# Convolution taps summed by accumulating DMAs, with matmul operands at round SBUF addresses

## The chip, the cores and the metric

The kernel runs on one core of a Trainium2 chip. Five engines work side by side: TensorE (PE, matmuls; PEld is its weight load), VectorE (DVE), ScalarE (ACT), GpSimd (POOL) and SyncE (SP, which here issues DMAs). The metric is the device time of one execution in microseconds, lower is better; the time before is the median of 3 runs.

## What is computed

A short causal convolution over the sequence (7 taps, one softmaxed set of taps for each of 8 groups of 24 channels), then a two-layer feed-forward with a clipped quadratic between its layers:

```python
x: (8, 4096, 192)   weight: (8, 7)   w_in: (192, 2048)   w_out: (2048, 192)
w = softmax(weight)                                     # over the 7 taps
conv[b, s, h, :] = sum_k w[h, k] * x_pad[b, s + k, h, :]  # 6 zeros in front
h = conv.reshape(32768, 192) @ w_in
g = where(h >= 1, h, where(h <= -1, 0, (h + 1)**2 / 4))
out = g @ w_out
```

## The kernel before

**Tiles and steps.** The 32,768 tokens form 64 blocks of 512 (`TB`), and `s` counts them. Each block has 8 steps (`NPAIR`), one for each 256 columns of the hidden layer, so the main loop runs over `q` = 0 to 511, and two more turns. In a step PE does the first layer for `q` (`mm1`, line 390) and the second layer for `q - 2` (`mm2`, line 430). The 192 channels are cut as 128 + 64, and every matmul is cut into two of 64 rows that run on the two halves of the array at once. Here such two are called a pair. From block 1 in the first layer, and from step 16 in the second, each operand is split into a high and a low part of type fp32r (`hi`/`lo`, `gh`/`gl`, `w`), and three products of parts are summed. A full step is 9 pairs in `mm1` and 10 in `mm2`, all with 512 columns. The moving operand of a pair is one row of 512 floats (2,048 bytes) in each partition: the convolved tokens in `mm1` (pool `xo`), `gh` and `gl` in `mm2` (pool `act`). The stationary operand is 128 floats (512 bytes) in each partition of `w0` to `w9` and `wr2` to `wr9` (pool `const`). In the first steps the operands are plain fp32, and lines 408 and 426 run on whole values.

**Between the layers.** For each `q`: DVE clips `h` from PSUM (line 463), ACT squares (469), DVE takes the maximum with `h` (474), and one step later ACT rounds to `gh` (481) and DVE subtracts to `gl` (487). After each block ACT copies four accumulators out, POOL adds them (501, 512), DVE transposes and SP stores.

**The convolution.** It is made for two blocks at a time, a unit `c` of 16 steps (`i` = 0 to 15), and ahead of its use. A unit has three parts, called B (the first 128 channels of the odd block), A (those of the even block) and R (the last 64 channels of both). Each part goes through: DVE transposes the loaded tokens to `xT` (147, "T" in the tables); ACT multiplies tap 0 into `y` (226); for each of taps 1 to 6 ACT makes a product `p` (219) and POOL adds it to `y` (230); "split" then makes the parts that matmuls read: ACT casts `y` to `hi` (248; for R `rh`, 262), POOL (for R DVE) subtracts to `lo`, and SP's DMAs copy both with the halves swapped. A and R made in unit `c` serve unit `c + 1`; B serves its own unit from `i` = 8 on. Three tables, `PLAN_B`, `PLAN_A` and `PLAN_R`, say at which `i` which taps are done; they are read in the order B, A, R, at the end of each step's work on ACT, POOL and DVE. All engines work their queues in order. Tiles `xT` and `y` have two buffers, `p` three. The first unit has tables of its own (`FIRST_...`) and another path (line 129), which the change leaves alone.

**Where tiles lie.** Pools are laid out in SBUF in the order in which they are opened, and tiles within a pool in the order in which they are first asked for. `w0` starts at byte 16,512 of each partition, which is 128 above a multiple of 512, and so do all parts of `w` and `wr`. All tiles of `xo`, `act` and `ob` start 448 bytes above a multiple of 1,024.

Of the kernel before, what the change touches and what calls it, by code (L numbers as in the profile page):

```python
# [8 lines left out]
F32 = mybir.dt.float32  # L9
# [5 lines left out]
ALU = mybir.AluOpType  # L15
# [3 lines left out]
P = 128  # L19
# [11 lines left out]
def lightconv_then_ffn(ctx: ExitStack, tc: tile.TileContext, x, weight, w_in, w_out, out):  # L31
# [24 lines left out]
    nc = tc.nc  # L56
    B, S, D = x.shape
    H, K = weight.shape
# [12 lines left out]

    const = ctx.enter_context(tc.tile_pool(name="const", bufs=1))
    stage = ctx.enter_context(tc.tile_pool(name="stage", bufs=2))
    xin = ctx.enter_context(tc.tile_pool(name="xin", bufs=3))
    xw = ctx.enter_context(tc.tile_pool(name="xw", bufs=2))
    xo = ctx.enter_context(tc.tile_pool(name="xo", bufs=3))
    act = ctx.enter_context(tc.tile_pool(name="act", bufs=2))
    ob = ctx.enter_context(tc.tile_pool(name="ob", bufs=2))
    ps_h = ctx.enter_context(tc.tile_pool(name="ps_h", bufs=2, space=PSUM))
    ps_o = ctx.enter_context(tc.tile_pool(name="ps_o", bufs=1, space=PSUM))  # L80
    ctx.enter_context(tc.manual_schedule())
# [53 lines left out]
    class Conv:  # L135
# [86 lines left out]
        def taps(self, *ks):  # L222
            y = self.y
            for k in ks:
                if k == 0:
                    nc.scalar.mul(y, self.xT[:, SH:SH + TB], wk[:, self.wsel, 0:1])
                elif self.c == 1 and self.u != "b":
                    pending.append((y, y, self.product(k)))
                else:
                    nc.gpsimd.tensor_add(y, y, self.product(k))  # L230

        def swapped(self, t, name, bufs):

# [35 lines left out]
        def split_halves(self):  # L269
# [26 lines left out]
    wo_w = w_out.bitcast(U32).rearrange("(f p) (d two) -> p f d two", p=P, two=2)  # L296
    n_in = [CI if j < NPAIR else 0 for j in range(NCH)]
    n_all = [n_in[j] + (CO if j >= LAG else 0) for j in range(NCH)]
    W = [const.tile([P, 2, n_in[j] + (CW if j >= LAG else 0)], F32R, name=f"w{j}")
         for j in range(NCH)]  # L300
    CC = max(n_all)
# [12 lines left out]
    class Chunk:  # L314
# [51 lines left out]
        def parts(self, rest):  # L366
            j, k = self.j, n_in[self.j]
            if rest:
                yield (WF[j][:, :, 0:P],
                       *(W[j][:, i, k:].rearrange("p (f d) -> p f d", f=2) for i in range(2)))  # L370
                yield WF[j][:, :, P:], WR[j][:, :, 0], WR[j][:, :, 1]
            else:
                yield WI[j], W[j][:, 0, 0:k], W[j][:, 1, 0:k]

# [15 lines left out]
    def mm1(q):  # L390
# [11 lines left out]
        else:  # L402
            mms = [(W[j][:, part], u + u, [xop[s][u, x]] * 2) for u in "nsr"
                   for part, x in ((0, "hi"), (1, "hi"), (0, "lo"))]
# [25 lines left out]
    def mm2(q):  # L430

        s, j = divmod(q, NPAIR)
        gh, gl = ghs.pop(q), gls.pop(q)
        w, wr, k = W[j + LAG], WR[j + LAG], n_in[j + LAG]
        if j == 0:
# [131 lines left out]
                    in_=y[i][:, 0:2 * D].rearrange("p (b d) -> p b d", b=2))  # L567


    wk = const.tile([P, 2, K], F32, name="wk")  # L570
    warm = const.tile([P, 1], F32, name="warm")
    whose = const.tile([P, 2 * P + 3 * K + 3], F32, name="whose")[:, 0:2 * P]
    one = ob.tile([P, TB], F32, name="sum")[:, 0:P]
    small, busy = (ob.tile([P, TB // SQ, SQ], F32, name="osb").rearrange("p j b -> p (j b)")
                    for _ in range(2))
# [118 lines left out]

    PLAN_B = {0: (0, 1), 2: (2, 3), 3: (4, 5), 4: (6,), 5: "split"}
    PLAN_A = {4: ("T", 0), 5: (1, 2), 6: (3, 4), 7: (5, 6), 8: "split"}
    PLAN_R = {7: ("T",), 8: (0, 1, 2), 10: (3, 4), 11: (5, 6), 13: "split"}


    FIRST_B = {2: 2, 3: 3, 4: 4, 5: 5}
# [4 lines left out]
    def conv_slot(i, b, a, r):  # L707
        early = b.c == 0
        plans = ((None if early else b, PLAN_B), (a, FIRST_A if early else PLAN_A),
                 (r, FIRST_R if early else PLAN_R))  # L710
        for u, plan in plans:
# [201 lines left out]
```

## Time and profile before

| | us |
|---|---|
| median of 3 runs | 2256.68 |
| lowest, highest | 2256.22, 2258.37 |
| span of the profiled execution, first to last instruction | 2255.6 |
| PE busy | 2249.6 |
| DVE busy | 2103.2 |
| ACT busy | 1697.6 |
| POOL busy | 1168.4 |

An engine's busy time is the time in which at least one of its instructions runs. The records of matmuls include the time in which a result drains out of the array, so successive ones overlap and a busy PE says nothing of the rate: that is read from how many matmuls end up in a stretch of time. A group's row gives the count, the busy time, the mean of one in ns, and the idle time of the engine just before them with what ended it. In a row of stretches each engine's busy time stands with the number of its instructions that touch the stretch.

### The profile page before, as it was taken

The numbers are of one execution on the slowest core, as the hardware profiler recorded it, in microseconds if no ns is written. First come the engines' busy times: TensorE is split into PE (matmuls) and PEld (weight loads), VectorE is DVE, ScalarE is ACT, GpSimd is POOL, SyncE is SP. The second block draws the span as 40 slices with busy tenths as digits, with TensorE's granted clock in tenths as the row PEclk, the third lists the DMA queues.
The fourth block names the chain that finished last, engine by engine and source line by source line (L and its number), as shares of the span: only waits on it lengthen the run. The fifth ranks groups of instructions, "written<-read, shape, count | busy, mean of one in ns | idle before, by whom it ended". The sixth has DMA issues, their size and how long they took to land.

```text
span 2255.6 us, 48202 instructions
## 1 busy us (share of the span) xinstructions
PE 2249.6 (100%) x19645; PEld 1842.2 (82%) x19645; DVE 2103.2 (93%) x1883; ACT 1697.6 (75%) x2153; POOL 1168.4 (52%) x868
## 2 busy tenths in 40 slices
PE   9999999999999999999999999999999999999999
PEld 6988888888888888888888888888888888888887
DVE  8899999999999999999999999999999999999997
ACT  7677877778777787777877777877778777787775
POOL 1446644556445565454654455644556545565441
PEclk9999999999999999999999999999999999999999
DMA  7222222222222212222222222222222222212211
GB/s 158 49 51 48 42 46 47 51 53 39 51 49 46 53 34 51 49 49 51 41 46 47 49 51 51 39 49 46 49 53 39 51 49 46 54 35 50 49 34 24
DMA packets 442125, 110.84 MB, mean 49 GB/s; under 512 B 410288, under 2 KB 417840, under 8 KB 441904
## 3 DMA queue, kind: packets, MB, share of 16 engines
q1 hardware_dynamic: 441744, 107.66, 25.8%
q8 instruction: 155, 2.54, 0.5%
q14 instruction: 66, 0.54, 0.1%
q10 hardware_dynamic: 160, 0.10, 0.0%
HBM read 32.84 MB, written 25.17 MB: 26 GB/s over the span
## 4 chain that ended last, share of the span: by engine, by line
PE 100%; ACT 0%; DVE 0%; issue 0%; DVEq 0%; POOL 0%; POOLq 0%; ACTq 0%
PE h L408 47%; PE accm L452 30%; PE accr L452 20%; PE accr L426 1%; PE accm L426 1%; PE accr L190 0%; PE accm L602 0%; PE accr L408 0%; PE accm L181 0%; PE h L155 0%; PE h L553 0%; PE accr L646 0%; ACT xT L168 0%; ACT xT L165 0%; ACT xT L167 0%
## 5 line engine op out<-in xcount | busy, mean ns | idle before, releaser
L230 POOL TENSOR_TENSOR y<-y,p 128x512 f32<-128x512 f32 x546 | 765.5, 1402 | 730.8 <-DVE g L474 559.5
L487 DVE TENSOR_TENSOR gl<-g,gh 128x1024 fp32r<-128x1024 f32 (+1 forms) x497 | 732.1, 1473 | 27.6 <-ACT gh L481 23.6
L469 ACT ACTIVATE g<-g 128x1024 f32<-128x1024 f32 (+1 forms) x505 | 535.3, 1060 | 242.4 <-DVE g L463 232.9
L463 DVE TENSOR_SCALAR g<-h 128x1024 f32<-128x1024 f32 (+1 forms) x505 | 609.8, 1208 | 97.1 <-PE h L408 88.1
L481 ACT CAST gh<-g 128x1024 fp32r<-128x1024 f32 (+1 forms) x497 | 521.7, 1050 | 237.1 <-DVE g L474 225.6
L408 PE MATMUL h<-hi,w 64*128 64x512 f32 x4032 | 629.8, 389 | 0.0
L474 DVE TENSOR_TENSOR g<-h,g 128x1024 f32<-128x1024 f32 (+1 forms) x505 | 613.4, 1215 | 12.1 <-ACT g L469 4.5
L452 PE MATMUL accm<-gh,w 64*128 64x512 f32 x3966 | 535.0, 388 | 0.0
L408 PEld LDWEIGHTS h<-hi,w 64*128 64x128 f32 x4032 | 382.6, 184 | 81.9
L452 PEld LDWEIGHTS accm<-gh,w 64*128 64x128 f32 x3966 | 372.3, 184 | 81.8 <-issue 0.2
L408 PE MATMUL h<-lo,w 64*128 64x512 f32 x2016 | 399.6, 388 | 0.0
L219 ACT ACTIVATE p<-xT,wk 128x512 f32<-128x512 f32 x562 | 375.1, 710 | 0.0
L452 PE MATMUL accm<-gl,w 64*128 64x512 f32 x1984 | 308.1, 388 | 0.0
L452 PE MATMUL accr<-gl,wr 64*128 64x512 f32 x1984 | 308.0, 388 | 0.0
L452 PE MATMUL accr<-gh,wr 64*128 64x512 f32 x1984 | 308.0, 388 | 0.0
L408 PE MATMUL h<-rh,w 64*128 64x512 f32 x992 | 306.0, 388 | 0.0
L408 PE MATMUL h<-rhi,w 64*128 64x512 f32 x992 | 306.0, 388 | 0.0
L408 PEld LDWEIGHTS h<-lo,w 64*128 64x128 f32 x2016 | 193.3, 184 | 41.5 <-DMA lo<-lo 0.3
L501 POOL TENSOR_TENSOR sum<-t 128x512 f32<-128x512 f32 (+1 forms) x124 | 160.7, 1316 | 126.3 <-ACT t L499 126.3
L452 PEld LDWEIGHTS accm<-gl,w 64*128 64x128 f32 x1984 | 186.4, 184 | 40.9
L452 PEld LDWEIGHTS accr<-gh,wr 64*128 64x128 f32 x1984 | 186.4, 184 | 40.9
L452 PEld LDWEIGHTS accr<-gl,wr 64*128 64x128 f32 x1984 | 186.4, 184 | 40.9
(145 smaller groups left out, 1976.8 us busy)
## 6 DMA issues: line engine op xcount, KB each, us to landing
out_dram<-osb SPq DMA_DIRECT2D x366, 64.0 KB, 2.0
raw<-in_x_dram SPq DMA_DIRECT2D x334, 68.0 KB, 2.4
hi<-hi SPq DMA_DIRECT2D x126, 128.0 KB, 2.3
lo<-lo SPq DMA_DIRECT2D x126, 128.0 KB, 2.3
rhi<-rh SPq DMA_DIRECT2D x62, 128.0 KB, 2.2
rlo<-rl SPq DMA_DIRECT2D x62, 128.0 KB, 2.3
words<-in_moe_w_in_dram SPq DMA_DIRECT2D x16, 192.0 KB, 4.0
words<-in_moe_w_out_dram SPq DMA_DIRECT2D x8, 384.0 KB, 5.0
```

The costliest lines, as they stand in the source:

```text
L219: nc.scalar.mul(p, self.xT[:, SH + k:SH + k + TB], wk[:, self.wsel, k:k + 1])
L230: nc.gpsimd.tensor_add(y, y, self.product(k))
L408: nc.tensor.matmul(h[e], w[HALVES[e], c0:c0 + P], x[e][e], start=(n == 0), stop=(n == len(mms) - 1))
L426: nc.tensor.matmul(accs[s][a, i][:, c0:c0 + D], g[half, e, b * P:(b + 1) * P], w[half, e, :], start=(j == 0 and e == 0 and b % 2 == 0), st ...
L452: nc.tensor.matmul(accs[s][a, i], st, g[HALVES[i], e, :], start=(j == 0 and n == first[a]), stop=(j == NPAIR - 1 and n == last[a]))
L463: nc.vector.tensor_scalar(out=g[:, e, :], in0=hs[q][:, e, :], scalar1=-1.0, scalar2=1.0, op0=ALU.max, op1=ALU.min)
L469: nc.scalar.activation(g[:, e, :], g[:, e, :], AF.Square, bias=0.5, scale=0.5)
L474: nc.vector.tensor_tensor(out=g[:, e, :], in0=h[:, e, :], in1=g[:, e, :], op=ALU.max)
L481: nc.scalar.copy(gh[:, e, :], gs[q][:, e, :])
L487: eng.tensor_sub(gl[:, e, :], g[:, e, :], gh[:, e, :])
L501: nc.gpsimd.tensor_add(y[:, n], t[0][:, n], t[1][:, n])
```

## The change

Two things are changed.

**The adds.** Line 230's add on POOL becomes a DMA issued from POOL's queue that reads `p` and adds it onto `y` in SBUF (`accum_op`). The three tables are spread: mostly one tap a step for each part instead of two, B's split moves from `i` = 5 to 6, A's from 8 to 10, R's from 13 to 14; A's transpose comes at 2 instead of 4.

**The addresses.** Pools `xw` and `xin`, whose tiles have odd sizes (`xT` and `raw` are 2,176 bytes), are opened after `ob`; `warm` and `wk` are asked for before the weights, with `warm` at 320 bytes; `whose` loses 96 bytes. With that `w0` starts at 16,896, a multiple of 512, as do all parts of `w` and `wr`, and all tiles of `xo`, `act` and `ob` start at multiples of 1,024. No matmul is added, removed or moved.

```diff
-    xin = ctx.enter_context(tc.tile_pool(name="xin", bufs=3))
-    xw = ctx.enter_context(tc.tile_pool(name="xw", bufs=2))
     xo = ctx.enter_context(tc.tile_pool(name="xo", bufs=3))
     act = ctx.enter_context(tc.tile_pool(name="act", bufs=2))
     ob = ctx.enter_context(tc.tile_pool(name="ob", bufs=2))
+    xw = ctx.enter_context(tc.tile_pool(name="xw", bufs=2))
+    xin = ctx.enter_context(tc.tile_pool(name="xin", bufs=3))
...
                 else:
-                    nc.gpsimd.tensor_add(y, y, self.product(k))
+                    nc.gpsimd.dma_start(out=y, in_=self.product(k), accum_op=ALU.add)
...
+    warm = const.tile([P, 80], F32, name="warm")[:, 0:1]
+    wk = const.tile([P, 2, K], F32, name="wk")
     W = [const.tile([P, 2, n_in[j] + (CW if j >= LAG else 0)], F32R, name=f"w{j}")
...
-    wk = const.tile([P, 2, K], F32, name="wk")
-    warm = const.tile([P, 1], F32, name="warm")
-    whose = const.tile([P, 2 * P + 3 * K + 3], F32, name="whose")[:, 0:2 * P]
+    whose = const.tile([P, 2 * P], F32, name="whose")
...
-    PLAN_B = {0: (0, 1), 2: (2, 3), 3: (4, 5), 4: (6,), 5: "split"}
-    PLAN_A = {4: ("T", 0), 5: (1, 2), 6: (3, 4), 7: (5, 6), 8: "split"}
-    PLAN_R = {7: ("T",), 8: (0, 1, 2), 10: (3, 4), 11: (5, 6), 13: "split"}
+    PLAN_B = {0: (0, 1), 1: (2,), 2: (3,), 3: (4,), 4: (5, 6), 6: "split"}
+    PLAN_A = {2: ("T", 0), 3: (1,), 4: (2,), 5: (3,), 6: (4,), 7: (5,), 8: (6,), 10: "split"}
+    PLAN_R = {7: ("T", 0), 8: (1,), 9: (2,), 10: (3,), 11: (4,), 12: (5, 6), 14: "split"}
```

How the queues change is shown at two places of a unit in the middle of the program. The first is POOL's queue from B's tap 1 (`i` = 0) to B's split. A row is a line of the program, an operation, what it writes and reads, and the semaphores that it waits for (DMASW are those of POOL's own DMAs, DMAHW those of SP's, the others name engines). Before:

```order
L230 TENSOR_TENSOR y<-y,p 128x512 [waits Activation_49]
L501 TENSOR_TENSOR sum<-t 128x512 [waits DVE_49,Activation_49] x2
L230 TENSOR_TENSOR y<-y,p 128x512 [waits Activation_49,Pool_49] x2
L512 TENSOR_TENSOR sum<-sum,t 64x512 [waits Activation_49]
L230 TENSOR_TENSOR y<-y,p 128x512 [waits Activation_49,Pool_49] x3
L252 TENSOR_TENSOR lo_8797<-y,hi_8796 128x512 [waits DMAHW4_49,DMAHW5_49,PE_49,Activation_49]
```

And after:

```order
L230 DMA y<-p 128x512 [waits Activation_49,Pool_49]
L503 TENSOR_TENSOR sum<-t 128x512 [waits DVE_49,Activation_49] x2
L230 DMA y<-p 128x512 [waits DMASW0_49,Activation_49]
L230 DMA y<-p 128x512 [waits DMASW1_49,Activation_49]
L514 TENSOR_TENSOR sum<-sum,t 64x512 [waits Activation_49]
L230 DMA y<-p 128x512 [waits DMASW2_49,Activation_49]
L230 DMA y<-p 128x512 [waits DMASW7_49,DVE_49,Activation_49]
L230 DMA y<-p 128x512 [waits DMASW3_49,Activation_49]
L230 DMA y<-p 128x512 [waits DMASW5_49,Activation_49]
L230 DMA y<-p 128x512 [waits DMASW4_49,Activation_49]
L230 DMA y<-p 128x512 [waits DMASW7_49,Activation_49]
L252 TENSOR_TENSOR lo_8853<-y,hi_8852 128x512 [waits DMAHW4_49,DMASW6_49,DMAHW5_49,PE_49,Activation_49]
```

The six adds of B are now six DMAs, each of which waits for the landing of the one before it on the same `y`; between them stand A's taps 1, 2 and 3. In the third and fourth row from below, B's tap 6 waits for tap 5, which was issued just before it, and A's tap 2 stands behind that wait.

The second place is ACT's queue from B's taps 5 and 6 to its split. Before:

```order
L219 ACTIVATE p<-xT,wk 128x512
L219 ACTIVATE p<-xT,wk 128x512 [waits Pool_49]
L481 CAST gh<-g 128x1024 [waits DVE_49,PE_49]
L469 ACTIVATE g<-g 128x1024 [waits DVE_49]
L219 ACTIVATE p<-xT,wk 128x512 [waits Pool_49]
L226 ACTIVATE y<-xT,wk 128x512 [waits DVE_49]
L481 CAST gh<-g 128x1024 [waits PE_49]
L469 ACTIVATE g<-g 128x1024 [waits DVE_49,Activation_49]
L248 CAST hi_8796<-y 128x512 [waits DMAHW3_49,DMAHW2_49,Pool_49]
```

And after:

```order
L219 ACTIVATE p<-xT,wk 128x512 [waits DMASW2_49,Activation_49]
L219 ACTIVATE p<-xT,wk 128x512 [waits DMASW3_49,Activation_49]
L219 ACTIVATE p<-xT,wk 128x512 [waits DMASW4_49,Activation_49]
L483 CAST gh<-g 128x1024 [waits DVE_49,PE_49]
L471 ACTIVATE g<-g 128x1024 [waits DVE_49]
L219 ACTIVATE p<-xT,wk 128x512 [waits DMASW5_49,Activation_49]
L483 CAST gh<-g 128x1024 [waits DVE_49,PE_49]
L471 ACTIVATE g<-g 128x1024 [waits DVE_49]
L248 CAST hi_8852<-y 128x512 [waits DMAHW3_49,DMAHW2_49,DMASW6_49]
```

B's cast to `hi` now waits for the landing of a DMA (tap 6) instead of for POOL's add, and stands two steps behind the products of taps 5 and 6. Each product also waits for the landing of a DMA: the one that last read its `p` buffer.

## The prediction

> **What bounds the kernel now.** I read the page's head and its chain of work first, then the granted clock.
>
> ```profile
> span 2255.6 us, 48202 instructions
> PE 2249.6 (100%) x19645; PEld 1842.2 (82%) x19645; DVE 2103.2 (93%) x1883; ACT 1697.6 (75%) x2153; POOL 1168.4 (52%) x868
> PE 100%; ACT 0%; DVE 0%; issue 0%; DVEq 0%; POOL 0%; POOLq 0%; ACTq 0%
> core 0: 2255.6 us, clock 1.000
> ```
>
> The chain that ended last lies on PE alone, at the full clock. So nothing that DVE, ACT, POOL or a DMA does is on the path now; only the pace of PE's matmuls is. That pace is not to be had from busy times. I take it from counts in long stretches (the columns: stretch, length, then each engine's busy time with its instructions; last the clock, the DMA share and GB/s).
>
> ```profile
> 200.00:1200.00 1000.00, 1000.00 (x8742) 819.97 (x8740) 942.39 (x806) 759.03 (x947) 536.08 (x385) 1.00 0.26 47
> 1200.00:2200.00 1000.00, 1000.00 (x8742) 819.98 (x8740) 941.77 (x806) 759.25 (x948) 537.02 (x382) 1.00 0.25 46
> 200.00:2200.00 2000.00, 2000.00 (x17480) 1639.95 (x17478) 1884.15 (x1611) 1518.28 (x1895) 1073.10 (x767) 1.00 0.26 47
> 104.00:2248.00 2144.00, 2144.00 (x18738) 1758.02 (x18736) 2013.71 (x1725) 1619.03 (x2017) 1134.23 (x811) 1.00 0.25 46
> ```
>
> The two halves together count 4 matmuls more than the whole, so each stretch counts 4 that only reach into it. 2000 us hold 17,476 half matmuls, 8,738 pairs: **228.9 ns a pair**, alike in both halves. 19 pairs make a step of 4.349 us. From 104 us to the end it is 18,734 / 2 = 9,367 pairs.
>
> Is 228.9 ns what 512 columns must take? The first steps run on plain fp32, with other column counts (columns of the timeline: start, length, engine, line, what, count):
>
> ```profile
> 15.27 1.88 PE L408 MATMUL h<-hi,gh 64*128 64x512 f32 x8
> 16.98 1.02 PE L408 MATMUL h<-rh,gh 64*128 64x512 f32 x4
> 17.84 1.88 PE L408 MATMUL h<-hi,gh 64*128 64x512 f32 x8
> 19.56 1.02 PE L408 MATMUL h<-rh,gh 64*128 64x512 f32 x4
> 20.41 0.82 PE L426 MATMUL accm<-wf,g 64*128 64x192 f32 x8
> 21.07 0.82 PE L426 MATMUL accr<-wf,g 64*128 64x192 f32 x8
> 21.71 0.82 PE L426 MATMUL accm<-wf,g 64*128 64x192 f32 x8
> 22.36 0.82 PE L426 MATMUL accr<-wf,g 64*128 64x192 f32 x8
> ```
>
> 12 pairs of 512 columns go from 15.27 to 20.41 us, 428.3 ns each; 12 pairs of 192 columns from 20.41 to 22.36 us, 162.5 ns each. The 320 columns between them cost 265.8 ns, 0.831 ns a column, and 162.5 - 192 x 0.831 leaves 3.0 ns fixed for a matmul. An fp32r pair needs 228.9 ns for the same 512 columns, about half, so I take it to stream at twice that rate: 512 x 0.4153 + 3.0 = **215.7 ns** (an estimate from these rows). Measured is 13.2 ns more, and it is there in every stretch. A gain must come out of these 13.2 ns, or there is none.
>
> The Trainium skill, "TensorE: Matmul & The Clock Gate", section "Back-to-back issue gap", gives N / 2.4 + 2.5 ns for successive matmuls, 215.8 ns at 512. The first steps' 3.0 ns agree with its fixed part, the 228.9 ns do not; by that page's gap the sum below would be 122 us instead of 124.
>
> **The change part by part.**
>
> *Addresses.* What could 13.2 ns be? A row of 512 floats is 2,048 bytes, read at 4 bytes per 0.4153 ns; 13.2 ns are then 127 bytes. The rows begin at 448 bytes above a multiple of 1,024, which is 3.5 x 128: if the array's reads go by blocks of 128 bytes, a row touches 17 of them where 16 would do, and one block more costs 13.3 ns. In the first steps a block lasts twice as long in the array as it takes to read, which would hide it there. At multiples of 1,024 the row has 16 blocks. The weights start at 128 above a multiple of 512, already whole blocks of 128, and load beside the matmuls (PEld 82%), so I expect nothing from their move. The cost of a matmul by address is nowhere in the trace of before, since every fp32r row lies at the same offset. The bounds are 13.2 ns less a pair and, if the new offsets were the worse ones, as much more: 9,367 x 13.2 ns = 124 us either way. I take the whole gain, because bytes and time agree within 1%: **-124 us**.
>
> *DVE, once PE is faster.* A step of 19 x 215.7 ns is 4.098 us. DVE is busy 1884.15 of 2000 us, 4.097 us a step: it would have nothing left. Here the adds matter.
>
> ```profile
> L487 DVE TENSOR_TENSOR gl<-g,gh 128x1024 fp32r<-128x1024 f32 x495 | 730.8, 1476 | 27.1 <-ACT gh L481 23.2
> L474 DVE TENSOR_TENSOR g<-h,g 128x1024 f32<-128x1024 f32 x503 | 612.2, 1217 | 12.1 <-ACT g L469 4.5
> L230 POOL TENSOR_TENSOR y<-y,p 128x512 f32<-128x512 f32 x546 | 765.5, 1402 | 730.8 <-DVE g L474 559.5 <-ACT p L219 147.7
> L501 POOL TENSOR_TENSOR sum<-t 128x512 f32<-128x512 f32 x122 | 158.7, 1321 | 123.3 <-ACT t L499 123.3
> L512 POOL TENSOR_TENSOR sum<-sum,t 64x512 f32<-64x512 f32 x61 | 138.3, 2268 | 1.5 <-ACT t L511 1.5
> L252 POOL TENSOR_TENSOR lo<-y,hi 128x512 fp32r<-128x512 f32 x62 | 81.1, 1308 | 144.4 <-ACT hi L248 144.4
> ```
>
> The subtraction to `gl` takes 1,476 ns, the maximum over as many elements 1,217. The timeline shows why: the subtraction that meets an add of POOL is slower.
>
> ```profile
> 998.73 1.30 POOL L230 TENSOR_TENSOR y<-y,p 128x512 f32<-128x512 f32 x1 [19.04 <-DVE g L474]
> 1000.51 1.22 DVE L487 TENSOR_TENSOR gl<-g,gh 128x1024 fp32r<-128x1024 f32 x1
> 1002.78 2.56 POOL L501 TENSOR_TENSOR sum<-t 128x512 f32<-128x512 f32 x2 [2.75 <-ACT t L499]
> 1004.86 1.56 DVE L487 TENSOR_TENSOR gl<-g,gh 128x1024 fp32r<-128x1024 f32 x1
> ```
>
> Without line 230, 158.7 + 138.3 + 81.1 = 378 of POOL's 1,144 us are left, a third, so of the 259 ns of excess I keep 86: DVE 0.173 us less a step, 3.92 of 4.098 us or 96%, where it has 94% now and holds up nothing. For the odd step with two transposes I add **+2 us**. The adds' own 765.5 us of POOL are off the path: nothing.
>
> *The DMAs.* 546 of them, 256 KB each.
>
> ```profile
> hi<-hi SPq DMA_DIRECT2D x126, 128.0 KB, 2.3
> words<-in_moe_w_out_dram SPq DMA_DIRECT2D x8, 384.0 KB, 5.0
> q1 hardware_dynamic: 441744, 107.66, 25.8%
> 1008.20 0.86 SPq L528 DMA_DIRECT2D out_dram<-osb  x2
> L219 ACT ACTIVATE p<-xT,wk 128x512 f32<-128x512 f32 x562 | 375.1, 710 | 0.0
> ```
>
> An accumulating one isn't in the trace. From issue to landing I bound it by 2.3 us (half the bytes, within SBUF) and 5.0 us (1.5 times the bytes, from DRAM, while the start loads everything), and take 3.0, near the first, which is the same kind of copy. The Trainium skill, "DMA: Bandwidth & Descriptors", section "Anatomy of one DMA", has about 2 us plus bytes / 436e3 for POOL's path, 2.6 us here; with it too the chains below fit. Issuing one costs POOL between the 0.43 us of SP's and the 1.30 us of an add, so POOL gets no busier. The load: 143 MB more beside 107.66 MB at 25.8% is 60% at most at the same cost per byte.
>
> What waits? POOL's queue stands behind tap 6's wait for tap 5 (A's tap 2 is behind it), and ACT's cast to `hi` in `i` = 6 waits for tap 6. From the start of tap 5's product in `i` = 4 to that cast are two steps, 8.20 us at the faster pace; less the product's 0.71 us, 7.5 us for two landings, 3.75 each. At 3.0 us there are 1.5 us to spare: nothing. R's taps 5 and 6 in `i` = 12 and its cast in 14 have the same distance. Single taps have a whole step, 4.1 us, each.
>
> **The sum.** 2255.6 - 124 + 2 = 2133.6 us of span; the median lies 1.1 us above this execution's span: **2135 us**.
>
> **The rivals.**
>
> *No effect of addresses.* The 13.2 ns belong to an fp32r matmul as such. For it: they are the same for all pairs in every stretch; against it: nothing but their size. Then PE stays the bound, the relief of DVE and POOL is off the path, and the time is 2256 us. The Trainium skill, "SBUF — State Buffer", section "Specifications (TRN2)", knows lines of 16 bytes; 448 is a multiple of 16, so by that page the move gives nothing. No row of before can decide it.
>
> *Half an effect*, the weights' reads or another block size holding the rest: about 2197 us.
>
> *Late chains: slower.* Where an accumulation takes longer than 3.75 us, ACT's in-order queue stands at the two casts, and behind it the square and `gh` that the next `mm2` needs. With L us to land, each of 31 units loses up to 2 x (2L - 7.5) us, less what ACT's idle quarter takes back. At L = 5.0, the upper bound, that is 155 us: 2290 us even with the full gain. Slower begins at L = 4.7. For it: 256 KB are read twice and written. Against it: the 2.3 us of the nearest copy.
>
> *Worse offsets: slower.* Weights and rows now begin at the same 512-byte phase; if that made them collide, up to +124 us, 2380 us.
>
> **How the numbers follow.** Forecast 0.45, half an effect 0.08, no effect 0.27, late chains 0.14, worse offsets 0.06. Faster by over 0.2% (what a measurement here can tell from no change) is 0.53; within it 0.26, a little of "no effect" falling outside; slower 0.21. The range takes in the forecast, with up to 15 us below for a smaller fixed part, the half effect and no effect, 0.80 together: 2120 to 2262 us. The forecast's own range is 2125 to 2160, the upper end for DVE as the bound.
>
> **What would show it.** Right: some 18,730 matmuls in 2,022 us, a pair at 215.7 ns, the first steps unchanged; the subtraction near 1.3 us; no idle time of ACT's casts on a DMA. Wrong: a pair still at 228.9 ns (no effect); PE with idle time behind `gh` or `hi` (late chains); PE idle behind DVE (the relief was too small).

## The result, and the profile after

The changed kernel takes **2479.08 us** (median of 4 runs, 2467.35 to 2487.02) against 2256.55 of before: 1.098 times the time, 95% interval 1.095 to 1.101. It is slower by a tenth, where I had forecast 2135 us.

The head of the page of after, its chain of work and its clock, in the order in which I read them before:

```profile
span 2485.2 us, 48615 instructions
PE 2%; issue 0%; DMA 0%; SPq 0%; POOL 0%; DVE 0%; ACT 0%; DVEq 0%; POOLq 0%
core 0: 2485.2 us, clock 0.972
```

The chain can be followed back through 2% of the span only, and DMAs and POOL stand in it: PE is no longer the one engine behind the end. The granted clock is down to 0.972. If PE had work all the time, the full clock would make the 2485.2 us about 70 us shorter (2485.2 x 0.028, an estimate). Who waits for what stands in the view of waits (engine, tile and line, the releaser, us in total, times, longest):

```profile
POOL y L230 <- DMA y<-p: 622.7, 232, 5.4
...
ACT rh L262 <- DMA y<-p: 75.3, 30, 5.2
...
ACT p L219 <- DMA y<-p: 53.8, 60, 1.8
...
PE h L410 <- DMA lo<-lo: 36.9, 29, 3.2
PE h L410 <- POOL lo L252: 35.4, 28, 2.8
...
PE h L410 <- DMA rhi<-rh: 20.4, 22, 2.4
PE h L410 <- DMA rlo<-rl: 16.5, 30, 0.7
...
PE accm L454 <- ACT gh L483: 9.2, 12, 1.3
```

Once a unit (there are 31) the first layer waits for the low part of B, and once a unit for R's two parts. Behind both stand the landings of the new DMAs: the cast to `rh` waits for one directly, and POOL's queue waits for one 232 times. The page's row on them, with KB each and the median time from issue to landing, and the queue's row (packets, MB, share):

```profile
y<-p POOLq DMA_DIRECT2D x546, 256.0 KB, 3.4
q0 software_dynamic: 78624, 143.17, 32.3%
```

3.4 us, not 3.0; one in twenty takes over 4.8 us. One unit shows how that becomes idle time of PE. POOL's timeline, then a piece of the timeline with PE, ACT and SP beside it (start, length, engine, line, what, count, and in brackets the idle time before it):

```profile
1113.27 0.86 POOL L230 DMA_DIRECT2D y<-p  x1 [2.35 <-DMA y<-p]
1117.00 1.76 POOL L230 DMA_DIRECT2D y<-p  x2 [2.87 <-ACT g L471]
1123.26 0.86 POOL L230 DMA_DIRECT2D y<-p  x1 [4.51 <-ACT gh L483]
1123.82 1.64 POOL L252 TENSOR_TENSOR lo<-y,hi 128x512 fp32r<-128x512 f32 x1
```

```profile
1120.53 0.60 ACT L248 CAST hi<-y 128x512 fp32r<-128x512 f32 x1
...
1123.13 0.61 PE L410 MATMUL h<-hi,w 64*128 64x512 f32 x4
...
1125.49 0.46 SPq L235 DMA_DIRECT2D lo<-lo  x1
...
1125.52 0.50 PE L410 MATMUL h<-lo,w 64*128 64x512 f32 x2 [1.77 <-POOL lo L252]
1125.85 0.63 PE L410 MATMUL h<-hi,w 64*128 64x512 f32 x4
...
1127.72 1.60 PE L410 MATMUL h<-lo,w 64*128 64x512 f32 x2 [1.24 <-DMA lo<-lo]
```

B's cast to `hi` ends at 1121.13. POOL could subtract `lo` then, but A's tap 3 stands ahead in its queue and waits for A's tap 2, the second issue in the 1.76 us row at 1117.00. The bracket at 1123.26 names ACT's cast, which is one of several things that this instruction waits for; in the trace tap 2 is issued at 1117.53 and lands 5.2 us later, at 1122.73, and tap 3 follows it by 0.53 us. So `lo` starts at 1123.82, 2.7 us late, and PE, which has reached the step that reads it, stands twice: first for `lo` itself, then for its copies. The windows view of the same place (stretch, length, five engines' busy time with counts, clock, DMA share, GB/s) shows the second half of the price:

```profile
1127.20:1128.50 1.30, 0.78 (x1) 0.28 (x1) 0.00 (x0) 0.68 (x1) 0.67 (x1) 0.50 0.53 123
1128.50:1131.50 3.00, 2.99 (x15) 2.41 (x16) 0.86 (x1) 0.00 (x0) 0.75 (x1) 0.50 0.46 83
...
1136.00:1141.00 5.00, 5.00 (x47) 5.00 (x46) 3.99 (x4) 3.40 (x6) 1.47 (x3) 1.00 0.55 99
```

The granted clock is 0.50 in the second gap and for some microseconds behind it, and the matmuls that do run take about twice as long. The trace of before has no such stretch.

For everything below I use one ledger. The trace gives the time from the first matmul of `mm1` in a step to that of the next step. Less 19 pairs at the kernel's own undisturbed spacing, that is what the step lost, the cost of the half clock included. The mean over units 1 to 30 of the profiled execution, by `i`:

| kernel | median us | lost, us a unit | at `i`=0 (R) | at `i`=6 | at `i`=8 (B) |
|---|---|---|---|---|---|
| before | 2256.6 | 0.05 | 0.01 | 0.00 | 0.00 |
| after | 2479.1 | 8.20 | 1.88 | 1.10 | 5.08 |
| addresses alone | 2235.7 | 0.05 | 0.01 | 0.00 | 0.00 |
| tables, adds on POOL | 2260.6 | 0.86 | 0.10 | 0.00 | 0.70 |
| DMAs and tables, old addresses | 2525.5 | 8.83 | 2.30 | 1.43 | 4.83 |
| only B by DMA | 2336.4 | 3.32 | 0.12 | 0.04 | 2.78 |
| only A by DMA | 2251.1 | 0.65 | 0.01 | 0.00 | 0.00 |
| only R by DMA | 2280.2 | 1.44 | 1.38 | 0.00 | 0.00 |
| `lo` on DVE | 2472.5 | 7.54 | 2.44 | 1.19 | 3.15 |
| half of each tap by DMA | 2418.3 | 5.76 | 0.31 | 0.07 | 5.21 |
| half, and `lo` on DVE | 2346.5 | 3.82 | 0.39 | 0.10 | 2.17 |

The steps between lose next to nothing in the changed kernel: three places hold 8.06 of its 8.20 us.

### The profile page after: what moved, and what is told of

Read it like the earlier page. It is cut to its first block, busy times and chain, and to the rows that moved or that the text cites. A ratio compares the mean times of both kernels' runs of the same rounds, so it can differ in the third digit from the quotient of the medians.

```text
span 2485.2 us, 48615 instructions
## 1 busy us (share of the span) xinstructions
PE 2352.8 (95%) x19645; PEld 1935.0 (78%) x19645; DVE 2047.4 (82%) x1883; ACT 1698.8 (68%) x2153; POOL 821.7 (33%) x868
## 5 line engine op out<-in xcount | busy, mean ns | idle before, releaser
L230 POOL DMA_DIRECT2D y<-p x546 | 474.1, 919 | 1385.7 <-DMA y<-p 622.7
L489 DVE TENSOR_TENSOR gl<-g,gh 128x1024 fp32r<-128x1024 f32 (+1 forms) x497 | 674.4, 1357 | 121.8 <-ACT gh L483 117.6
L410 PE MATMUL h<-hi,w 64*128 64x512 f32 x4032 | 747.4, 388 | 4.2 <-DMA hi<-hi 4.2
L410 PE MATMUL h<-lo,w 64*128 64x512 f32 x2016 | 606.4, 398 | 73.6 <-DMA lo<-lo 36.9
L454 PE MATMUL accm<-gh,w 64*128 64x512 f32 x3966 | 658.3, 401 | 9.8 <-ACT gh L483 9.2
L410 PEld LDWEIGHTS h<-hi,w 64*128 64x128 f32 x4032 | 538.7, 185 | 70.8 <-DMA hi<-hi 6.3
L454 PEld LDWEIGHTS accm<-gh,w 64*128 64x128 f32 x3966 | 471.9, 191 | 89.8 <-ACT gh L483 21.2
L410 PEld LDWEIGHTS h<-lo,w 64*128 64x128 f32 x2016 | 349.5, 186 | 140.0 <-DMA lo<-lo 61.5
L454 PE MATMUL accm<-gl,w 64*128 64x512 f32 x1984 | 416.1, 400 | 2.0 <-DVE gl L489 0.3
L454 PE MATMUL accr<-gh,wr 64*128 64x512 f32 x1984 | 407.7, 393 | 0.0
L410 PEld LDWEIGHTS h<-rhi,w 64*128 64x128 f32 x992 | 182.0, 188 | 49.2 <-DMA rhi<-rh 31.4
```

Source lines behind the costliest of these rows:

```text
L230: nc.gpsimd.dma_start(out=y, in_=self.product(k), accum_op=ALU.add)
L410: nc.tensor.matmul(h[e], w[HALVES[e], c0:c0 + P], x[e][e], start=(n == 0), stop=(n == len(mms) - 1))
L454: nc.tensor.matmul(accs[s][a, i], st, g[HALVES[i], e, :], start=(j == 0 and n == first[a]), stop=(j == NPAIR - 1 and n == last[a]))
L489: eng.tensor_sub(gl[:, e, :], g[:, e, :], gh[:, e, :])
```

## The experiments

### Addresses, DMAs and tables apart

The new addresses, with line 230's add and the three tables of before:

```diff
-                    nc.gpsimd.dma_start(out=y, in_=self.product(k), accum_op=ALU.add)
+                    nc.gpsimd.tensor_add(y, y, self.product(k))
```

> The new addresses with the adds on POOL and the old tables, so no accumulating DMA. Theory S (the addresses are worth 2.2 ns a pair, as the changed kernel's 226.67 ns in its undisturbed stretches say): 9,367 pairs x 2.2 ns = 21 us off 2256.6, about 2236 us, ratio 0.991, PE in the chain throughout, clock 1.00. Rival T (the addresses are worth the forecast 13.2 ns, and 143 MB of DMA traffic beside the matmuls hides most of it in the changed kernel): pairs at 215.7 ns, about 2135 us. Rival D (the pairs are faster but DVE, at 942 of 1000 us, can't follow): above 2240 us with PE waiting for DVE.

2235.73 us, ratio 0.991 (0.989 to 0.992): theory S to the microsecond, and **faster than both kernels**, 0.9% below before. Its windows and the clock:

```profile
200.00:1200.00 1000.00, 1000.00 (x8828) 826.47 (x8826) 946.29 (x814) 763.01 (x955) 538.82 (x385) 1.00 0.25 48
1200.00:2200.00 1000.00, 1000.00 (x8828) 826.46 (x8826) 944.11 (x811) 762.41 (x954) 540.45 (x383) 1.00 0.24 46
```

8,824 half matmuls in 1000 us are 4,412 pairs, 226.65 ns each (the records, in whole ns, give 226.67). The gain is 2.2 ns a pair, not 13.2, and no DMA traffic hid the rest.

The DMAs and the spread tables in the kernel of before:

```diff
-                    nc.gpsimd.tensor_add(y, y, self.product(k))
+                    nc.gpsimd.dma_start(out=y, in_=self.product(k), accum_op=ALU.add)
```

> The accumulating DMAs and the spread tables at the old addresses. Theory C (the loss is the late chains: a landing of 3.4 us and 0.5 us to the next issue leave single taps no slack): pairs at 228.9 ns where nothing disturbs, PE waiting for the lo and rh parts as in the changed kernel, about 2256.6 + 240 = 2490 to 2500 us, some 20 us more than the changed kernel's. Rival (the loss comes from the new addresses, or from both together): near 2257 us.

2525.52 us, ratio 1.119 (1.117 to 1.120). The loss is the DMAs' and tables'; it comes out 25 us above the top of what I expected, with the same three places in the ledger.

The changed kernel with line 230's add alone put back, so that only tables and addresses differ from before:

> The new addresses and the spread tables, but each tap added by POOL. Theory C: the spread tables do no harm by themselves, so the time is that of the addresses alone, 2236 us within 5 us, and no part is late. Rival (the tables put the parts too late whoever adds): more than 2300 us, PE waiting for the lo parts and for rh.

2260.60 us, ratio 1.002 (1.001 to 1.003). A miss for both theories: the tables do cost, 24.9 us over the addresses alone, most of it ahead of B's low part. PEld's wait in this run:

```profile
PEld h L410 <- DMA lo<-lo: 19.6, 33, 1.7
```

Here no accumulating DMA exists. B is late because its split stands in `i` = 6 instead of 5. Counted from the start of `mm1` in `i` = 6, the mean times in B's path (units 1 to 29) are:

| kernel | `hi` ends | `lo` starts | `lo` ends | `mm1` of `i`=8 starts |
|---|---|---|---|---|
| addresses alone | 1.71 | 1.79 | 3.09 | 8.61 |
| tables, adds on POOL | 6.08 | 6.16 | 7.46 | 8.61 |
| only B by DMA | 7.74 | 8.18 | 9.47 | 8.85 |
| `lo` on DVE | 7.96 | 8.49 | 9.17 | 9.83 |
| half of each tap by DMA | 6.49 | 8.84 | 10.38 | 8.68 |
| half, and `lo` on DVE | 6.49 | 7.40 | 8.44 | 8.74 |
| after | 7.85 | 9.80 | 11.44 | 9.72 |

After `lo` come two copies on SP, the second issued 0.5 us behind the first; with the tables alone it lands 3.0 us after the end of `lo` in the mean. The third pair of `mm1` reads `lo` itself, but the copies are read first by the sixth pair, at 8.61 + 5 x 0.227 = 9.74 us. So `lo` must end by about 6.7 us. The old table leaves 3.6 us to spare; the new one is 0.76 us late before a DMA has taken any time, which is close to the 0.70 us of the ledger.

### One part at a time by DMA

In each of these kernels one part keeps its DMAs and its new table; the others are added by POOL. With A or R alone, the other two also have their old tables back; with B alone, they keep the new ones. The edit for B:

```diff
-                    nc.gpsimd.dma_start(out=y, in_=self.product(k), accum_op=ALU.add)
+                    if self.u == "b":
+                        nc.gpsimd.dma_start(out=y, in_=self.product(k), accum_op=ALU.add)
+                    else:
+                        nc.gpsimd.tensor_add(y, y, self.product(k))
```

> The changed kernel with A's and R's taps added by POOL again; only B's six taps are DMAs. In the changed kernel PE loses 5.1 us a unit ahead of the low part of B, 1.1 us two steps before, and 2.0 us ahead of R's. Theory C1 (B's own chain of six landings is too long): the 5.1 us stay, about 2235 + 31 x 5.1 = 2390 us. Rival C2 (it is the other parts' taps in POOL's queue, and their waits, that hold B up): the gap ahead of B's low part is down to the 0.7 us of the tables alone, about 2260 us. R's loss goes in both.

2336.37 us, ratio 1.034 (1.033 to 1.036), between the two. Ahead of B's low part PE loses 2.78 us a unit: 0.70 the tables', so about 2.1 B's own six landings. The other 2.3 of the changed kernel's 5.08 come with A's and R's DMAs. B's own lateness is seen at its cast:

```profile
ACT hi L251 <- DMA y<-p: 39.6, 31, 2.6
```

1.3 us a unit, and `hi` ends 1.66 us later than with POOL's adds (7.74 against 6.08).

A alone:

> The changed kernel with only A's taps as DMAs, by the spread table; B and R go back to POOL's adds and their old tables. A's parts are read from the next unit's first step on, six steps after its last tap, so it is the one part with time to spare. Theory C (a landing costs only where the chain has no slack): 2236 us within 4, as with the addresses alone, with PE never idle. Rival (accumulating DMAs cost by their traffic, their issue on POOL or their waits in POOL's queue, wherever they stand): 186 of them at the changed kernel's loss of 243 us for 546 make 83 us, 2319 us.

2251.10 us, ratio 0.997 (0.996 to 0.998): much nearer to 2236 than to 2319, but 15 us off. A's parts are not late. What is lost is lost in `i` = 10 (0.43 us a unit) and 13, on other work, and not by A's new table, with which POOL's adds lose nothing there:

```profile
ACT p L219 <- DMA y<-p: 26.3, 26, 3.0
...
PE accm L457 <- ACT t L503: 5.8, 8, 2.4
```

A landing holds one of the three `p` buffers, the next product waits for it at the head of ACT's queue, and the copies that free PE's accumulators stand behind. So slack of the part itself does not make a landing free.

R alone:

> The changed kernel with only R's taps as DMAs, by its spread table; B and A by POOL's adds and their old tables. In the changed kernel PE loses 1.9 us a unit ahead of R's parts. Theory own chain: the 1.9 us stay, 2236 + 31 x 1.9 = 2295 us. Rival queue (R was late only behind B's and A's waits): 2236 to 2245 us.

2280.24 us, ratio 1.010 (1.008 to 1.012). The time is nearer to the 2295 us of its own chain. R loses 1.38 of its 1.88 us by itself, so most of it is its own chain, and its cast is where it waits:

```profile
ACT rh L265 <- DMA y<-p: 59.3, 30, 4.2
```

The loss of 1.10 us at `i` = 6 is in none of the three runs, so it needs the DMAs of more than one part. In the changed kernel PE's 12 waits for `gh` are all at `i` = 6, and ACT's 60 waits for a `p` buffer are all at `i` = 5 and 6, while its casts wait for landings only at `i` = 7, 15 and 0 (all counted by PE's steps). This points to the `p` buffers; no run tests it, with more of them for instance.

### The chain's length, or the place in POOL's queue

B's and A's `lo` on DVE instead of POOL:

```diff
-                    u.split()
+                    u.split(nc.vector)
```

> The changed kernel with the subtraction to lo of B and A taken from POOL to DVE, so that it doesn't stand behind another part's tap in POOL's queue. Theory C (the chain itself ends too late): lo comes 1 to 2 us sooner in each of 31 units, with the half clock behind it up to 100 us, at most: 2400 to 2450 us, and PE's gap before lo stays over 2 us a unit. Rival Q (what costs is only that lo stands behind waits for landings in POOL's queue): the gap before lo goes, about 2479 - 31 x 6 = 2290 us.

2472.50 us, ratio 1.095 (1.094 to 1.097). The gap ahead of B falls from 5.08 to 3.15 us, as theory C has it, but the time hardly moves and stays above theory C's 2400 to 2450 us: R loses 0.56 us more, and 0.6 us appear in `i` = 10 to 13. Two runs now give POOL's queue a like share of B's loss: 1.9 us here, 2.3 us with B alone. Both figures include the half clock, which comes with the longer gaps: step `i` = 8 runs at 0.50 for 4.1 us a unit in the changed kernel, for 1.5 us here and for 0.8 us with B alone. As the half clock loses at most half of its time, up to 1.3 of the 1.9 us and up to 1.6 of the 2.3 us can be the clock's.

Half the bytes a landing, in the same number of landings:

```diff
-                    nc.gpsimd.dma_start(out=y, in_=self.product(k), accum_op=ALU.add)
+                    p, n = self.product(k), TB // 2
+                    nc.gpsimd.dma_start(out=y[:, 0:n], in_=p[:, 0:n], accum_op=ALU.add)
+                    nc.gpsimd.tensor_add(y[:, n:], y[:, n:], p[:, n:])
```

> The changed kernel, in which each tap's first 256 columns are accumulated by the DMA and the other 256 are added by POOL, right behind the DMA's issue: half the bytes a landing, the same number of landings, the same tables. In the changed kernel the first packet moves 1.44 us after the issue and the landing comes at 3.4 us; if the rest goes with the bytes, a landing takes about 2.4 us. Theory C (six landings in a row are too long for the tables): the cycle of a tap falls from about 4.2 to 3.0 us, under a step, the lateness of the first taps is caught up, and PE's loss falls from 8.2 us a unit to 1 to 3 us: 2265 to 2330 us. Rival F (a landing's time is mostly fixed, not by bytes): 3.1 us or more a landing and 2450 us or more. Rival N (the number of waits in POOL's queue decides, not their length): 2450 us or more though the landing is shorter.

2418.27 us, ratio 1.071 (1.069 to 1.073), out of theory C's range and below that of both rivals.

```profile
y<-p POOLq DMA_DIRECT2D x546, 128.0 KB, 2.7
```

A landing is 0.8 us shorter (medians 3.44 and 2.65 us before rounding; I had expected 2.4), and with that the losses at R's parts and at `i` = 6 are all but gone (0.31 and 0.07 us). B's is not: `hi` now ends at 6.49 us, but `lo` starts only at 8.84, behind A's taps and their new halves on POOL. With `lo` on DVE as well:

> Both at once: half of each tap by DMA and half by POOL, and B's and A's lo subtracted on DVE. With whole taps, lo on DVE took 1.9 us from the gap of 5.1 us a unit ahead of B's low part; with half taps alone the gap stayed at 5.2 us, while the losses at R's parts and two steps ahead of B's fell from 3.0 to 0.4 us. Theory C+Q (the chain's length and lo's place behind A's taps in POOL's queue each suffice to make B late, so neither cure shows alone): the gap falls to 0 to 1.5 us a unit, 2240 to 2290 us. Rival (B's chain is still too long at 2.7 us a landing): the gap stays over 3 us, 2340 us or more.

2346.53 us, ratio 1.040 (1.038 to 1.041): the time is in the rival's range, the gap of 2.17 us in neither. It falls from 5.21 us, the half clock included, so `lo`'s place was the larger share there. What stays comes from the table (`hi` ends at 6.49 us, where 6.08 was already too late) and from DVE's queue, in which `lo` waits 0.9 us more. On DVE `lo` also holds up `gl`; that PE waits for `gl`, mostly at `i` = 12, is new:

```profile
PE h L412 <- DMA lo<-lo: 28.1, 35, 1.8
PE accm L456 <- DVE gl L491: 18.2, 19, 2.5
```

### Which address counts

All of these are the kernel of the addresses alone, with tiles moved by the order of the pools or the size of an unused tail. Weights back at 128 above a multiple of 512 (`warm` and `wk` asked for after the weights):

> The kernel of the addresses alone, with the weights back at 128 above a multiple of 512 and the activations still at multiples of 1,024. If the moving rows' offset makes the difference: pairs at 226.67 ns, about 2236 us. If the weights' offset does: 228.9 ns, 2257 us. If each has a share: between them.

Weights at multiples of 512, activations back at 448:

> The other half: weights at multiples of 512, activations back at 448 above a multiple of 1,024. If the moving rows' offset makes the difference: 228.9 ns a pair, 2257 us. If the weights' offset does: 226.67 ns, 2236 us.

2289.68 and 2298.99 us: neither half gives a share, **both are slower than before**. The windows of the first and of the second:

```profile
200.00:1200.00 1000.00, 1000.00 (x8610) 809.85 (x8608) 923.81 (x794) 749.49 (x940) 541.54 (x383) 1.00 0.24 47
200.00:1200.00 1000.00, 1000.00 (x8574) 835.77 (x8572) 922.82 (x789) 746.08 (x934) 523.38 (x381) 1.00 0.25 47
```

4,303 pairs, 232.4 ns, and 4,285 pairs, 233.4 ns; over all steps the means are 232.38 and 233.33. So the two operands' addresses act together, and I moved them against each other:

> The addresses alone, both shifted by the same 128 bytes: weights at 128 above a multiple of 512, activations at 128 above a multiple of 1,024. So far: weights and activations (above a multiple of 512) at 0 and 0 give 226.67 ns a pair, 128 and 448 give 228.89, 128 and 0 give 232.38, 0 and 448 give 233.33. Theory R (what counts is how the two lie to each other): 226.67 ns, 2236 us. Rival A (each must be at a round address by itself): above 228 ns, 2250 us or more.

> Weights at multiples of 512, activations at 512 above a multiple of 1,024. If 512 is the period of what counts: 226.67 ns, 2236 us. If activations need multiples of 1,024: above 228 ns, 2250 us or more.

> Addresses alone, weights at multiples of 512, activations 256 above one. Rows of a pair so far by the distance of activations above weights, modulo 512: 0 gives 226.67 ns, 320 gives 228.89, 384 gives 232.38, 448 gives 233.33. If the loss grows towards 512 and starts above some distance (the moving row's end runs into something): 226.67 ns, 2236 us. If every distance but 0 costs: 228 ns or more, 2248 us or more. If the floor is not at 0: under 226 ns.

> As before this one, with activations 64 above a multiple of 512. If the loss grows towards 512: 226.67 ns, 2236 us. If every distance but 0 costs, or the loss is the same on both sides of 0 (448 is 64 below): 228 to 234 ns, 2250 to 2300 us.

| weights, activations (above a multiple of 512) | distance modulo 256 | ns a pair | us |
|---|---|---|---|
| 0, 0 | 0 | 226.67 | 2235.73 |
| 128, 128 | 0 | 226.67 | 2236.18 |
| 0, 0 (512 above 1,024) | 0 | 226.67 | 2236.05 |
| 0, 256 | 0 | 226.67 | 2235.72 |
| 0, 64 | 64 | 228.89 | 2256.76 |
| 128, 448 (before) | 64 | 228.89 | 2256.68 |
| 128, 0 | 128 | 232.38 | 2289.68 |
| 0, 448 | 192 | 233.33 | 2298.99 |

Eight placements, and one number orders them: how far activations lie from weights, modulo 256 bytes. Theory R was right, with a shorter period than I had tested for first. Six of the eight kernels were timed once; 13 runs of before lie within 0.1% of each other. Distances 128 and 192 rest on one kernel each. k4's loss where 448 had been worse also ends the idea that both sides of 0 are alike.

### Pairs of 256 columns

The list of products has another order in this kernel, so that the short pair stands second of three; of the edit, the matmul itself:

```diff
...
-                nc.tensor.matmul(h[e], w[HALVES[e], c0:c0 + P], x[e][e],
+                b = slice(0, TB // 2 if s and n % 3 == 1 else TB)
+                nc.tensor.matmul(h[e][:, b], w[HALVES[e], c0:c0 + P], x[e][e][:, b],
```

> The kernel of the addresses alone, in which one of the three products of parts in the first layer (weights' high part by the tokens' low part) is left out for the second half of the tokens: 3 of the 9 pairs have 256 columns. The other pairs stay at 226.67 ns. Theory per column (the row is read at 226.67 / 512 = 0.443 ns a column): a pair of 256 columns takes 113 to 115 ns. Theory fixed (0.4153 ns a column, 3.0 ns, and 10.9 ns once for each fp32r pair): 256 x 0.4153 + 13.9 = 120 ns. Rival (the load of the weights sets the pace, 94 ns of busy time a load): anything above 125 ns. Three pairs save 3 x 110 ns of a step of 4.307 us; the time falls to about 2090 us if nothing else becomes the bound, DVE (3.78 us a step) near it.

The start of one step's first layer in the timeline:

```profile
301.26 0.61 PE L411 MATMUL h<-hi,w 64*128 64x512 f32 x2
301.49 0.27 PE L411 MATMUL h<-lo,w 64*128 64x256 f32 x1
301.60 0.39 PE L411 MATMUL h<-hi,w 64*128 64x512 f32 x1
301.71 0.27 PE L411 MATMUL h<-lo,w 64*128 64x256 f32 x1
301.82 0.63 PE L411 MATMUL h<-hi,w 64*128 64x512 f32 x3
```

In 431 of 501 steps the matmul behind the step's first short one starts after 113 or 114 ns, half of 226.67: there the cost goes by the column, and nothing is charged once a pair. After that the two halves of the array run out of step, and matmuls of 512 columns follow each other on a half after 224 to 240 ns in most cases, 233 at the median, though the addresses are the good ones. PE also waits 12.6 us for ACT's copies of the accumulators. So 2173.53 us were reached, not 2090. Why halves out of step are slower stays open.

## Why the prediction was wrong, point by point

- **What bounds the kernel**: right for before. The addresses alone keep PE in the chain throughout and move the time with the pair.
- **Addresses, -124 us**: the sign was right, the size six times too large, and the reason wrong. Blocks of 128 bytes would make the time go by the row's own offset, whatever the weights do; but rows at 0 take 226.67 or 232.38 ns and rows at 448 take 228.89 or 233.33, as the weights lie. The sign was luck: the rows' move, to which I gave the whole gain, costs 33 us by itself, and only with the weights' move does it gain. The step that failed in the size is the estimate of 215.7 ns: it took half of the fp32 rate for what an fp32r pair can reach, but 226.67 ns is the least in every placement that I ran, and the short pairs show the 11.0 ns left as a cost of each column. The measured term is 9,367 x 2.2 ns = 21 us. That "I expect nothing" from the weights' move was wrong too: moving one operand alone costs 33 or 42 us. The Trainium skill, "SBUF — State Buffer", section "Specifications (TRN2)", has lines of 16 bytes, and all eight placements keep to multiples of 16, so by that page nothing sets them apart. The runs do, by up to 6.7 ns a pair.
- **DVE**: the relief came. The subtraction to `gl` takes 1,357 ns where it took 1,476 (forecast near 1,300), and it was off the path, since PE never came to 215.7 ns. The second row below is POOL's issues of the DMAs, at 919 ns within the bounds of the prediction:

```profile
L489 DVE TENSOR_TENSOR gl<-g,gh 128x1024 fp32r<-128x1024 f32 (+1 forms) x497 | 674.4, 1357 | 121.8 <-ACT gh L483 117.6
L230 POOL DMA_DIRECT2D y<-p x546 | 474.1, 919 | 1385.7 <-DMA y<-p 622.7 <-DVE g L476 391.1 <-ACT gh L483 117.5
```

- **The DMAs, "nothing"**: this is the step that decided. Of the 344 us between forecast and result, 101 lie in the addresses (2235.73 against 2135) and 243 in DMAs and tables. It failed in three ways. *The deadline.* I asked only whether tap 6 lands before the cast in `i` = 6, and never when the cast's result is needed. B's split a step later was an edit costed at nothing; it alone turns 3.6 us of slack into 0.76 us of lateness (tables: 24.9 us). *The landing.* (By the formula for POOL's path in the Trainium skill, "DMA: Bandwidth & Descriptors", section "Anatomy of one DMA", the estimate is 2.6 us; the accumulating DMA here takes 3.4.) 3.4 us instead of 3.0 is within the bounds, but to it comes about 0.53 us until POOL issues the next one on that `y`: taps 5 and 6, at 1113.27 and 1117.00, lie 3.7 us apart with the shortest of landings (3.2 us), and the issue at 1123.26 comes 5.7 us after the one that it waits for. The whole step of "single taps have a whole step" was then nearly used up (3.97 of 4.31 us at the median), so the wait for the accumulators' copies and sums at the unit's start was never caught up. Halving the bytes cured R and `i` = 6, which shows that the length of a landing counts there. *The queue.* I named A's tap 2 behind B's tap 6, but not `lo` behind A's tap 3: 1.9 to 2.3 us of B's 5.1, the half clock behind it included.
- **The rival of late chains** had the right kind of mechanism with the wrong place and point. By its formula 2 x 3.4 = 6.8 us is below 7.5 and nothing would be lost. R's cast does wait, as it said (75.3 us in 30 waits), but B is lost at `lo`, behind the cast.
- **The clock**: nothing in the prediction allowed for it. About 70 of the 251 us by which the changed kernel's span exceeds that of the addresses alone (2485.2 - 2234.2) lie in the granted clock, by the estimate from its mean above.

Worked together: 31 units at 8.2 us are 254 us, less 21 us for the pairs, 233; the spans of the two profiled executions differ by 229.6 (2485.2 - 2255.6). A table that starts B's chain early enough for its landings was not tried.

## What to carry to other kernels

A step that is moved later has its price at the first reader of its last result, so follow the chain through cast, subtraction and copies to that reader before calling the slack enough. An operation with a long fixed latency in a chain must be counted with its pick-up time in an in-order queue, and everything behind it in that queue, and every buffer that it holds, waits with it. A rate that no trace shows is a hypothesis: test the one edit by itself first, and here the better half of the change alone was the kernel to keep.

## What was not expected of the hardware

- A pair's time depends on the distance of its two operands' addresses modulo 256 bytes: 226.67, 228.89, 232.38 and 233.33 ns at 0, 64, 128 and 192.
- The granted clock halves at PE's longer gaps. The changed kernel has 28 stretches at 0.50, of 3.4 or 6.8 us, 136.5 us in all, of which 25 begin at `i` = 8.
- An accumulating DMA issued right behind another takes POOL 1.2 instead of 0.86 us to issue, and lands 4.1 instead of 3.2 us later (medians of 89 and 457 in the changed kernel; at most 6.4 and 5.5).
- Issuing DMAs on POOL does not slow DVE: in the changed kernel `gl` takes 1,213 ns with POOL idle, 1,214 beside an issue, and 1,697 in the mean beside one of POOL's adds or subtractions.
